# Chunk 5's squares sooner, chunk 1's tokens added on VectorE, and a transposition of the first group copied by ScalarE

## The chip, the core and the metric

The kernel runs on one core of a Trainium2 chip. The core has five engines with queues of their own: TensorE (PE) multiplies matrices into PSUM; VectorE (DVE) does elementwise work, reductions and transpositions of 32x32 blocks; ScalarE (ACT) does activations and copies; GpSimd (POOL) does elementwise work on SBUF; SyncE (SP) issues most of the DMAs. The metric is the device time of one execution in microseconds (us), lower is better. Beside it a profiled execution gives a trace; its span is the time from the first to the last instruction.

## What is computed

Two blocks follow each other. The first is a delta-rule attention over batch 4, 8 heads, 768 tokens and head size 48: a state matrix per head is read with each query, then corrected with each key and value.

```python
k_n = k / (np.linalg.norm(k, axis=-1, keepdims=True) + 1e-06)
for t in range(S):
    y[:, :, t] = np.einsum('bhd,bhde->bhe', q[:, :, t], state)
    v_old = np.einsum('bhde,bhd->bhe', state, kt)
    state = state + bt[:, :, :, None] * np.einsum('bhd,bhe->bhde', kt, vt - v_old)
```

The heads of a token then stand side by side as one row of 384 numbers, 3072 rows in all, and pass a feed-forward network with w_in (384 x 2048) and w_out (2048 x 384), both given in double precision:

```python
h = x @ w_in
g = 0.5 * h * (1.0 + erf(h * inv_sqrt2))
out = g @ w_out
```

## The kernel before

**Tiling.** The 768 tokens are cut into 12 chunks of 64. Two batches of 8 heads make a unit of 128 rows (`tiles[c, a]`, a = 0 and 1, so `NA` is 2), and two chunks make a group. Within a chunk the recurrence becomes a triangular system. Its Gram matrices come from PE (`grams`, L414, copied out by ACT in L425). The 32x32 diagonal blocks of a group are inverted together on DVE: `eliminate_steps` scales (L476, L477), flips (L482, L487), eliminates row after row (L496, L501, L503), and in `back` transposes the result three times: into `XM` (L512) and into the right and left columns of `Zf` (L516). In groups after the first the third of these is a copy by ACT instead (L520). `clear` then sets the lower left block of `Zf` to zero in group 0. The off-diagonal block is joined in two levels of small matmuls: `join` (L548, used for group 0) multiplies one 32x32 block at a time; `join_run` (L593, used for later groups) takes two heads at once and uses only the blocks it needs, in four strided pieces. Level 0 is scaled back into `XM` by DVE (L559 or L605), level 1 goes to `Zf` by ACT (L563 or L572).

**A chunk.** `against_state` multiplies keys and queries with the state (psK, L667), `subtract` forms the right side W (DVE, L678 and L684) and copies the part of the queries to y (ACT, L679), `solve` multiplies with Zf (psU, L702) and ACT copies U out, `use` and `update` form psY (L732, L743). `next_state` adds to the state (DVE, L748), and `read` gets the tokens x out of PSUM: for chunks 0 and 1 ACT copies them (L756), for later chunks DVE adds y in the same step (L758). `turn` transposes x for the network (psX); for chunk 1 it does so with two matmuls per 128 columns that add x and y on the way (L776), otherwise with one transposition (L779).

**Norms.** For chunks from 4 on, `norms` squares the keys on ACT (ksq), and `prep` sums the squares on DVE (L349) and takes the root on POOL (L351). `finish` turns both roots of a group into the factors gm on DVE (L303 to L307), which the group's elimination needs.

**The network.** For chunks 0 and 1 it is plain (psH with a gelu on ACT, L811 and L817 or L902; psO, L829). From chunk 2 on, `part_of_layer` and `second_layer` use fewer products with sums around them (L916, L859); L939, L947, L958 and L968 are DVE's sums between these products, and PE's next product into psY waits for L947. The weights arrive in double precision and are decoded to single by DVE and ACT during chunks 0 and 1: `begin` (L231, L234), `exponents` (L237, or ACT through the helper at L902), `mantissas` (L251, L253), `signed` (L260, L261), which also fetches a later part.

**Order.** Up to L1172 all engines run in the order in which the code is written. After that `plan` gives each step a time in units of chunks; the steps are sorted by it. DVE runs in exactly that order, and so do ACT's instructions that go through `keep` (L902); the others are placed by a scheduler. `together` holds PE's instructions of several steps together.

## Time and profile before

| what | value |
| --- | --- |
| median of 3 executions | 646.0 us (645.03 to 646.12) |
| profiled execution | 644.96 us |
| its span | 643.2 us |
| PE busy | 617.9 us, 96% |
| DVE busy | 496.3 us, 77% |
| ACT busy | 259.9 us, 40% |
| POOL busy | 66.0 us, 10% |
| mean granted clock of TensorE | 0.985 |

In a timeline each row has a start and a duration in us, the engine, the line of the kernel, the operation, what it writes and reads, and in brackets how long the engine had been idle before it and what ended that. Rows of one kind that follow closely are merged (x3), and a matmul counts as two records. In a view of waits the columns are: who waited for whom, us in total, how often, the longest. In a view of windows each row has the stretch, its length, then for PE, the loading of weights, DVE, ACT and POOL the busy time and the number of instructions, then the granted clock, the share of DMA and GB/s. In the clock row of the page each digit is a fortieth of the span, in tenths of full speed.

### The profile page before, as it was taken

To read this page: it belongs to the slowest core of one execution; us is meant where nothing else is said; L and a number is where in the kernel's file an instruction comes from. 1 tells how busy PE (TensorE), PEld (TensorE's weight loads), DVE (VectorE), ACT (ScalarE), POOL (GpSimd) and SP (SyncE) were. 2 spreads that over 40 slices of the span, in tenths; PEclk is the share of its full clock that TensorE was granted. 3 is DMA by queue.
4 is the path that set the end of the run, shared out by engine and by line. 5 is a ranking of instruction groups with operands and counts; after the bars stand their busy time and mean duration, and the time that the engine had idled before them with its cause. 6 is when DMAs were issued, how large, how long until landed. Compare 5 with 4: busy or idle time off the path is not lost.

```text
span 643.2 us, 22156 instructions
## 1 busy us (share of the span) xinstructions
PE 617.9 (96%) x9702; PEld 573.8 (89%) x9702; DVE 496.3 (77%) x1011; ACT 259.9 (40%) x586; POOL 66.0 (10%) x58
## 2 busy tenths in 40 slices
PE   6759999999989999999999999999999999999997
PEld 5658876776879999999999999999999999999997
DVE  6999989989589997999577999577999565354342
ACT  4576767524632256132266132266132253132230
POOL 4044002001301003001003001013001000000000
PEclk9987999999989999999999999999999999999999
DMA  9794683204422335312325312411211400100100
GB/s 135 174 273 159 129 199 113 45 1 74 84 37 42 56 43 91 58 24 37 66 34 86 61 21 41 67 21 33 51 25 35 69 3 3 25 2 3 25 2 24
DMA packets 158433, 39.79 MB, mean 62 GB/s; under 512 B 150016, under 2 KB 153216, under 8 KB 158336
## 3 DMA queue, kind: packets, MB, share of 16 engines
q1 hardware_dynamic: 155664, 37.34, 30.0%
q10 hardware_dynamic: 2672, 1.03, 0.8%
q8 instruction: 76, 1.25, 0.8%
q14 instruction: 21, 0.17, 0.1%
HBM read 33.62 MB, written 4.72 MB: 60 GB/s over the span
## 4 chain that ended last, share of the span: by engine, by line
PE 77%; DVE 14%; DMA 2%; issue 2%; SPq 2%; ACT 1%; POOL 1%; DVEq 0%; POOLq 0%
PE psX L859 12%; PE psY L916 11%; PE psY L859 8%; PE psX L916 8%; PE psV L916 5%; PE psZ L916 5%; PE psZ L859 4%; PE psV L859 4%; PE psK L667 3%; DVE Nu L503 3%; DVE tmp L501 3%; PE psG L414 3%; PE psJ L593 3%; PE psH L811 2%; PE psY L732 2%
## 5 line engine op out<-in xcount | busy, mean ns | idle before, releaser
L916 PE MATMUL psX<-xT,w_in_sb 128*128 128x128 f32 x480 | 64.8, 278 | 0.0
L503 DVE TENSOR_TENSOR Nu<-Nu,tmp 128x58 f32<-128x58 f32 (+13 forms) x168 | 57.9, 344 | 5.8
L501 DVE TENSOR_TENSOR tmp<-Nu 128x58 f32<-128x58 f32 (+13 forms) x168 | 58.0, 345 | 4.4
L916 PEld LDWEIGHTS psX<-xT,w_in_sb 128*128 128x128 f32 x480 | 59.4, 193 | 0.9
L902 ACT COPY xT<-psX 128x768 f32<-128x768 f32 x9 | 7.2, 799 | 124.3 <-PE psX L788 124.3
L351 POOL TENSOR_TENSOR n<-n,half 128x16 f32<-128x16 f32 x10 | 31.4, 3145 | 251.8 <-DVE n L349 191.2
L859 PE MATMUL psX<-w_out_sb,G 128*128 128x192 f32 x320 | 55.3, 326 | 0.0
L859 PEld LDWEIGHTS psX<-w_out_sb,G 128*128 128x128 f32 x320 | 52.1, 190 | 0.0
L811 PE MATMUL psH<-xT,w_in_sb 128*128 128x256 f32 x192 | 45.2, 390 | 0.5 <-ACT G L902 0.4
L829 PE MATMUL psO<-w_out_sb,G 128*128 128x384 f32 x128 | 43.9, 490 | 0.0
L811 PEld LDWEIGHTS psH<-xT,w_in_sb 128*128 128x128 f32 x192 | 36.3, 193 | 8.0 <-ACT G L902 1.3
L916 PE MATMUL psY<-xT,w_in_sb 128*128 128x128 f32 x320 | 43.1, 279 | 0.0
L916 PEld LDWEIGHTS psY<-xT,w_in_sb 128*128 128x128 f32 x320 | 39.8, 196 | 0.0
L902 ACT COPY pu<-psZ 128x512 f32<-128x512 f32 x40 | 23.5, 587 | 39.3 <-PE psZ L916 37.7
L829 PEld LDWEIGHTS psO<-w_out_sb,G 128*128 128x128 f32 x128 | 23.6, 190 | 14.0
L902 ACT ACTIVATE G<-G 128x512 f32<-128x512 f32 x40 | 25.2, 630 | 23.3 <-DVE G L947 22.6
L939 DVE TENSOR_TENSOR psY<-psY,pu 128x512 f32<-128x512 f32 x20 | 14.0, 698 | 22.4 <-PE psY L916 19.6
L376 POOL TENSOR_TENSOR V<-V,n 128x384 f32<-128x384 f32 x18 | 17.0, 959 | 135.4 <-DMA V<-in_v_dram 115.5
L859 PE MATMUL psZ<-T,pu 128*128 128x192 f32 x160 | 28.6, 332 | 0.0
L859 PE MATMUL psY<-T,G 128*128 128x192 f32 x160 | 28.6, 332 | 0.0
L859 PE MATMUL psV<-w_out_sb,G 128*128 128x192 f32 x160 | 27.7, 326 | 0.0
L859 PE MATMUL psX<-T,G 128*128 128x192 f32 x160 | 27.6, 326 | 0.0
(183 smaller groups left out, 1346.1 us busy)
## 6 DMA issues: line engine op xcount, KB each, us to landing
Kp<-in_k_dram SPq DMA_DIRECT2D x76, 96.0 KB, 3.2
w_out_sb<-in_moe_w_in_dram SPq DMA_DIRECT2D x24, 256.0 KB, 4.1
w_raw<-in_moe_w_out_dram SPq DMA_DIRECT2D x16, 384.0 KB, 4.5
V<-in_v_dram SPq DMA_DIRECT2D x48, 96.0 KB, 3.1
out_dram<-o_sb SPq DMA_DIRECT2D x40, 96.0 KB, 2.2
Qp<-in_q_dram SPq DMA_DIRECT2D x64, 32.0 KB, 2.1
Qp<-in_q_dram SPq DMA_DIRECT2D x16, 96.0 KB, 4.7
Qp<-in_k_dram SPq DMA_DIRECT2D x32, 32.0 KB, 2.2
```

What stands on the lines that cost most here:

```text
L351: nc.gpsimd.tensor_tensor(flat, flat, half, op=ALU.pow)
L376: engine.tensor_tensor(u.V, u.V, ns[u.c][:, u.a].unsqueeze(2).to_broadcast([128, H, D]), op=ALU.mult)
L414: nc.tensor.matmul(psG[HALF[p], r, i * NP + j, :], lhsT=u.Kt[rows, p, j, :], rhs=(u.Qt if x else u.Kt)[rows, p, j, :], start=True, stop=True)
L501: nc.vector.tensor_tensor(tmp, nu[:, j + 1:, j:j + 1].to_broadcast([128, n, j]), nu[:, j:j + 1, 0:j].to_broadcast([128, n, j]), op=ALU.mult)
L503: nc.vector.tensor_tensor(nu[:, j + 1:, 0:j], nu[:, j + 1:, 0:j], tmp, op=ALU.add)
L593: nc.tensor.matmul(psJ[HALF[p], k, :], lhsT=(xm if level else off)[rows, us, :], rhs=zf[rows, us, HB:C] if level else xm[rows, us, :], sta ...
L667: nc.tensor.matmul(u.psK[to, x, r, j, :], lhsT=(u.Qt if x else u.Kt)[rows, p, j, :], rhs=St[rows, u.a, p ^ r, j, :], start=True, stop=True)
L811: nc.tensor.matmul(psH, lhsT=w_in_sb[:, f // 2, m, f % 2 * 128:(f % 2 + 1) * 128], rhs=xTs[c][:, m, :], start=(m == 0), stop=(m == NM - 1))
L829: nc.tensor.matmul(u.psO, lhsT=G[:, u.a, f, :], rhs=w_out_sb[:, f, :], start=(f == 0), stop=(f == NF - 1))
L859: nc.tensor.matmul(ps_, lhsT=lhs[:, f, :], rhs=rhs[:, f, :], start=first and f == 0, stop=f == FH - 1, skip_group_check=not first)
L902: i = fn(*args, **kw)
L916: nc.tensor.matmul(ps_[:, i], lhsT=lhs[:, f // 2, f % 2 * 128:(f % 2 + 1) * 128], rhs=rhs, start=first and i == 0, stop=True, skip_group_c ...
```

## The change

Three things change.

- The third transposition of group 0 on DVE is left out. `turned_corner` copies the upper left block of `Zf` from its right columns on ACT instead, for chunk 0 before its second join level and for chunk 1 at time 1.05.
- Chunk 1's joins go through `join_run`, two heads at a time, with four instructions on DVE and four on ACT. Chunk 1's tokens are read as in later chunks: DVE adds y to them, and `turn` transposes once. For that the queries' product with the state is written to the partitions of the later chunks.
- Chunk 5's `norms` moves from time 3.06 to 2.93, and its `prep` from 3.06 to 2.961. In ACT's order the two squares now stand right behind the copies of xT of chunk 2, ahead of the Gram copies of chunk 4; in DVE's order the two sums stand ahead of L939 and L968. On SP, the loads of the keys of chunk 6 then stand ahead of one block load instead of behind it.

```diff
+    def turned_corner(c):
+        us = slice(c * NA * H, (c + 1) * NA * H)
+        for p in range(2):
+            top = slice(p * C, p * C + HB)
+            nc.scalar.copy(Zf[0][top, us, 0:HB], Zf[0][top, us, HB:C])
...
-                    psJ = small[0].tile([128, 512], F32, tag="sq" if level else "z", name="psJ")
+                    psJ = small[0].tile([128, 512], F32, tag="sq" if level or g == 0 else "z",
+                                        name="psJ")
...
-                        put_off("join", zf[p * C:p * C + HB, us, HB:C], src)
+                        put = put_off if g else lambda name, to, at: nc.scalar.copy(to, at)
+                        put("join", zf[p * C:p * C + HB, us, HB:C], src)
...
-                        to = HALF[p ^ (j % 2)] if x and u.c > 1 else HALF[p]
+                        to = HALF[p ^ (j % 2)] if x and u.c > 0 else HALF[p]
...
-            if u.c < 2:
+            if u.c < 1:
                 copy(dst, src)
...
-            if u.c == 1:
-
-                for i, part in enumerate((u.x, u.y)):
-                    nc.tensor.matmul(psX[:, m, :], lhsT=part.rearrange("q h d -> q (h d)")[:, cols],
-                                     rhs=ident, start=i == 0, stop=i == 1)
-            else:
-                nc.tensor.transpose(psX[:, m, :], u.x.rearrange("q h d -> q (h d)")[:, cols], ident)
+            nc.tensor.transpose(psX[:, m, :], u.x.rearrange("q h d -> q (h d)")[:, cols], ident)
...
     for a in range(NA):
         join(0, (a,), 0)
-    back2[0](*back2[1:])
+    turned_corner(0)
...
-             [(t, (join, 0, range(NA, 2 * NA), level)) for level, t in enumerate((1.085, 1.16))],
+             at(1.05, 1.051, [(1.0, turned_corner, 1)]),
+             [(1.085, (join_run, 0, range(NA, 2 * NA), ())),
+              (1.16, (join_run, 0, (), range(NA, 2 * NA)))],
...
-                         at(w + 0.06, w + 0.061, [(1.0, norms, 5), (1.0, prep, 5)]),
+                         at(w - 0.07, w - 0.069, [(1.0, norms, 5)]), at(w - 0.039, w - 0.038, [(1.0, prep, 5)]),
```

## The prediction

> **What bounds the kernel now.** I read the page first: how busy each engine is, and at which clock.

> ```profile
> span 643.2 us, 22156 instructions
> ...
> PE 617.9 (96%) x9702; PEld 573.8 (89%) x9702; DVE 496.3 (77%) x1011; ACT 259.9 (40%) x586; POOL 66.0 (10%) x58
> ...
> PEclk9987999999989999999999999999999999999999
> ```

> TensorE (PE) carries the time; the dips of the clock row (a slice is 16.1 us) say that it was slowed around 32 to 64 us and near 180. Then the waits of PE, longest first. After the start-up loads they are few, and from 180 us to the end none above 0.2 us is listed, so whatever PE gains before 180 us stays gained unless VectorE (DVE) then fails to keep up.

> ```profile
> PE psY L916 <- DVE G L947: 4.0, 1, 4.0
> ...
> PE psJ L548 <- DVE XM L559: 2.0, 2, 1.5
> ...
> PE psJ L593 <- DVE XM L512: 0.5, 1, 0.5
> ```

> The 4.0 us wait, in the timeline:

> ```profile
> 169.84 0.94 ACT L902 ACTIVATE ksq<-Kp 128x384 f32<-128x384 f32 x2
> ...
> 170.40 1.01 DVE L349 TENSOR_REDUCE n<-ksq 128x8 f32<-128x384 f32 x2 [0.30 <-ACT ksq L902]
> ...
> 171.33 1.75 DVE L842 TENSOR_TENSOR T<-w_out_sb,T 128x1536 f32<-128x1536 f32 x1
> ...
> 171.49 4.35 POOL L351 TENSOR_TENSOR n<-n,half 128x16 f32<-128x16 f32 x1 [10.76 <-DMA Kp<-in_k_dram]
> ...
> 175.87 0.18 DVE L303 TENSOR_SCALAR n<-n 128x32 f32<-128x32 f32 x1 [2.79 <-POOL n L351]
> ...
> 179.27 0.68 DVE L947 TENSOR_TENSOR G<-psY,pu 128x512 f32<-128x512 f32 x1
> ...
> 180.01 1.56 PE L916 MATMUL psY<-TX,w_in_sb 128*128 128x128 f32 x8 [4.00 <-DVE G L947]
> ```

> Chunk 5's squares (ksq) run on ScalarE (ACT) behind chunk 4's Gram copies; their sums, then the square root on GpSimd (POOL), follow; DVE stands 2.79 us before L303, and L947, whose psY was ready at 173.35 (172.29 + 1.06), queues behind. PE waits for L947. (The DMA named at POOL's row is a load of the next chunk; what released it is the sum that ends at 171.41.) The windows around it show the second price:

> ```profile
> 177.20:180.60 3.40, 0.59 (x5) 0.59 (x6) 3.33 (x5) 0.61 (x2) 0.60 (x1) 1.00 0.43 50
> 180.60:184.00 3.40, 3.40 (x19) 3.40 (x18) 3.33 (x5) 1.09 (x3) 0.00 (x0) 0.50 0.38 45
> ```

> After a stretch with PE busy 0.59 of 3.40 us the clock is 0.50 for 3.4 us. The 24 records from 180.01 take 4.41 us (the next group starts at 184.42); at 0.1115 each (8 in 0.89 later on) they are 2.68. So the wait costs 4.0 + 1.7 = 5.7.

> The other edits sit where PE and DVE are balanced:

> ```profile
> 45.00 1.94 DVE L516 STREAM_TRANSPOSE Zf<-Nu 128x1024 f32<-128x1024 f32 x1
> ...
> 63.51 0.35 ACT L902 ACTIVATE G<-psH 128x256 f32<-128x256 f32 x1
> ...
> 86.79 0.56 DVE L748 TENSOR_TENSOR St<-St,psY 128x384 f32<-128x384 f32 x1 [1.21 <-PE psY L743]
> ...
> 87.72 0.56 DVE L748 TENSOR_TENSOR St<-St,psY 128x384 f32<-128x384 f32 x1 [0.38 <-PE psY L743]
> ...
> 132.14 5.32 PE L829 MATMUL psO<-w_out_sb,G 128*128 128x384 f32 x16
> ...
> 135.71 2.09 DVE L512 STREAM_TRANSPOSE XM<-Nu 128x1024 f32<-128x1024 f32 x1
> ...
> 137.95 1.15 PE L593 MATMUL psJ<-XM,G 32*64 32x64 f32 x32 [0.48 <-DVE XM L512]
> ```

> At 87.7 DVE waits for PE. From there to 137.8 DVE decodes weights and eliminates without a gap above 0.21 us, and PE waits for it at 137.95. From 138 to 176 PE runs without a wait.

> [...] half for about 3.4 us after the 4.0 us wait, and for four windows from 44.5 to 58.1. [...] The root takes 2.90 us at 157.82 and 4.35 beside L842 at 171.49[...].

> **Squares sooner.** Nothing is removed: two squares (0.94), two sums (1.01) and one root move. ACT's order has the squares right after xT's second copy (162.62 + 0.48 = 163.1); ACT then idles until 164.56, so they end at 164.05 in its gap. Their input was loaded by issues at 149.6 to 153.5, a median 3.2 us to landing. On DVE the sums now stand behind L846 (ends 165.83): 166.85, in the 2.77 us before L939 at 168.60. The root then ends between 169.8 (2.90) and 171.2 (4.35). DVE goes L939, L968 (to 170.1), L842 (1.75, to 171.85), L303 at once: 4.0 earlier than 175.87. L947 ends at 179.95 - 4.0 = 175.95, and PE's preceding psV ends at 176.0. The wait closes and the dip with it: **-5.7**. POOL's queue holds nothing between the two roots. On SP the loads into the same K buffers, 171.00 before, no longer wait for the squares, and one block load goes behind them; PE waits for neither.
> Will DVE keep up? It starts 4.0 earlier, PE 5.7. Its next idle times are 0.93 (before L939 at 186.48) and 0.38 (L678 at 190.25); absorbed, it is 5.3 earlier. Its next hand-over is XM, ready at 228.36 for a PE that comes at 228.77: 0.4 spare. 5.7 - 5.3 = 0.4: just enough, cost 0 to 0.4; I take 0.

> **Third transposition.** DVE loses 1.94 us at 45.00. ACT gets four copies 32x512 (0.62 each, by diag<-G L425): two between 43.2 and 45.32, where it waited 2.30 us for psJ, and two behind the exponents that end at 56.2, before the gelu that PE releases at 58.34. Cost nothing there; without that cover 1.24 each pair. POOL's clearing starts about 1.2 sooner, but psU (47.76) needs ACT's clearing too, which ends 47.66 as before: no gain for chunk 0. DVE's decoding runs about 1.6 earlier (exponents on ACT at 54.50 hold the rest). So exponents of part 3 on ACT go from 61.50 to 60.03 (behind the gelu 59.64 + 0.39), end 62.17; L261 62.2 to 63.15.

> **Joins in pairs.** 32 records of 64 columns for 64 of 32: 1.15 for 1.20, nothing. DVE 4 x 0.43 = 1.74 (L605) for 1.41: +0.33. ACT 1.49 for 1.17, in idle time before the next gelu. XM then ends at 63.17 + 1.74 = 64.9 instead of 66.08, and PE, whose tile before it no longer waits behind ACT, is 1.1 earlier up to 86.5 (0.5 to 1.6).

> **Chunk 1's tokens.** PE drops 12 psX matmuls pairwise (1.34 per tile) for 3 transpositions (about 0.3): -2.1. ACT drops 6 copies, 1.96. DVE gets 6 adds, by L758 1.08 per tile, and behind them stands the decoding. At 87.7 DVE now does St, adds, St, adds: 85.65 + 2 x 1.58 (by 157.66 to 160.80) = 88.8 to 88.95, before 88.28. **+0.7** (0.2 to 1.3), carried by the full DVE queue to XM: 138.5 instead of 137.81. ACT's exponents, now behind earlier gelus, are within 0.1 of DVE's need once; 0 to 0.5 more.
> What is late next: PE would be done at 137.46 - 1.1 - 2.1 = 134.3, so it stands 3.5 to 4 us before this join, as long as the wait that vanishes at 176. If a clock window falls mostly into it, up to 3.4 us at half follow: 0 to 1.7. [...] I take half of it, **+0.9**, as what a median of executions sees.

> Sum against its own time (span 643.2, execution 644.96): -5.7 + 0.7 + 0.9 = -4.1, span 639.1, execution 640.9. That execution lies 1.04 under the median 646.0 of runs spread over 1.1[...]; from the median: **641.9**.

> **Rivals.**
> - *Full gain:* the stall before group 1's join doesn't slow the clock and DVE's lateness is 0.2. Speaks for it: earlier holes of 2 us left the clock at 1.00. 646.0 - 5.5 = 640.5.
> - *Small gain:* the dip comes whole, ACT's exponents add 0.5, DVE at 228 lags 0.4, adds 1.3: -5.7 + 1.3 + 0.5 + 0.4 + 1.7 = -1.8, 644.2. All ends at once; each is possible.
> - *It doesn't do what it says:* the root isn't what holds L947. Then only the start-up moves, and the 4.0 us of slack at 176 swallow it: 645.5 to 646.5. Against: the chain of waits passes root, L303, L947 in a row.
> - *Slower:* the clock stays at half after group 1's join for several windows, as it did for four at 44.5, because small matmuls (psJ, psK) follow the stall. PE is the bound from 138 on, so each window costs 1.7. It decides from three windows (5.1 against a net gain of 5.0); with four 646.0 - 5.0 + 6.8 = 647.8. Against: psO's large matmuls follow 3.1 us later.

> **How the numbers follow.** Forecast 0.58 (641.9, its own range 640.8 to 643.4), full gain 0.14, small gain 0.13, no change 0.06, slower 0.09. Below 0.2% (1.3 us) this kernel's measurement can't tell a change. Faster by more: 0.58 + 0.14 + 0.13 = 0.85; within: 0.06; slower 0.09. The range takes forecast, full and small gain: 639.8 to 644.6; left out are no change and slower, 0.15.

> **What would show it.** Squares right: POOL's root of chunk 5 before 168, L303 about 4 us sooner in its stage, no PE wait at L947's product and clock 1.00 after it. Transposition and joins: PE's psJ of chunk 1 near 65, the state update of chunk 1 near 85.6. Tokens: XM of group 1 0.2 to 1.3 later than 137.8, PE waiting 3 to 4 us there, the clock row telling whether a dip follows. The prediction is wrong if DVE reaches that join earlier than before, if a new PE wait above 1 us stands at 228, or if L303 still waits for POOL.

## The result, and the profile after

The changed kernel takes 644.32 us in the median of 14 runs (642.56 to 646.57) where the kernel before takes 645.78 (645.03 to 646.63): a ratio of 0.9973, 95% interval 0.9963 to 0.9982, so 1.5 us faster. The forecast was 641.9, 4.1 faster. The direction was right, the gain about a third of the forecast. The runs of the changed kernel spread over 4.0 us, those of the kernel before over 1.6.

The profiled execution took 644.23 us, 0.73 less than that of before (644.96). The page, first the lines that answer those of before:

```profile
span 642.5 us, 21992 instructions
...
PE 619.7 (96%) x9620; PEld 574.2 (89%) x9620; DVE 496.9 (77%) x1018; ACT 260.1 (40%) x586; POOL 64.5 (10%) x58
...
PEclk9567999989999999999999999999999999999999
```

PE is busy 1.8 us more than before, though it has 82 instructions fewer. PE's products take longer at half clock (32 records of psK 1.07 to 1.10 us there, 0.65 to 0.68 at full): the dip near 180 us (the twelfth slice of the row) is gone, but one has come in the ninth slice, 129 to 145 us. The lower digits of the start-up are no slower start-up: four transpositions of psT take 1.11 us from 20.38 us here and 1.11 us from 19.77 us before, at half the pace of those at 37.65 us before and 38.75 us here (a record every 0.21 and every 0.11 us). The trace of before names no clock ahead of its first change at 33.8 us, and its row shows full digits there. So the mean clocks of the two executions, 0.985 and 0.962, can't be compared. The waits of PE, whole span:

```profile
PE psJ L600 <- DVE XM L512: 2.9, 1, 2.9
...
PE psG L414 <- issue: 1.7, 2, 1.2
```

Before, the longest wait after the start-up was that for L947's product (L949 now), 4.0 us. It is no longer in the list. In its place stands the wait of group 1's join for XM, 2.9 us instead of 0.5. One of the two waits named "issue" (the engine waited for nothing that the profile shows) lies at 250 us; it returns below.

The stage of chunk 5's squares in the timeline (start, length, engine, line, operation):

```profile
167.22 0.94 ACT L904 ACTIVATE ksq<-Kp 128x384 f32<-128x384 f32 x2
...
169.97 1.01 DVE L349 TENSOR_REDUCE n<-ksq 128x8 f32<-128x384 f32 x2
...
171.05 2.90 POOL L351 TENSOR_TENSOR n<-n,half 128x16 f32<-128x16 f32 x1 [6.10 <-DVE n L349]
175.90 0.18 DVE L303 TENSOR_SCALAR n<-n 128x32 f32<-128x32 f32 x1
...
179.30 0.68 DVE L949 TENSOR_TENSOR G<-psY,pu 128x512 f32<-128x512 f32 x1
...
180.07 1.12 PE L918 MATMUL psY<-TX,w_in_sb 128*128 128x128 f32 x8
```

These clock times look like those of before, 175.9 for L303 and 180.1 for PE. But PE came to this stage 4.2 us later (the product at 164.36 before starts at 168.59 now), so relative to its stage everything here is 4.2 us sooner: the root ends 1.95 us ahead of L303, which doesn't wait, and PE doesn't wait for L949. In the windows from 177.20 to 184.00 PE is busy 3.40 of each 3.40 us at clock 1.00. So the part of the change with the largest price did all that was expected of it; the loss lies ahead of it, at group 1's join, where two small products follow each other, psJ (the join) and psK (keys and queries with the state):

```profile
130.80 5.32 PE L831 MATMUL psO<-w_out_sb,G 128*128 128x384 f32 x16
139.07 1.64 PE L600 MATMUL psJ<-XM,G 32*64 32x64 f32 x32 [2.95 <-DVE XM L512]
140.64 1.10 PE L675 MATMUL psK<-St,Kt 48*64 48x48 f32 x32
141.53 1.07 PE L675 MATMUL psK<-St,Qt 48*64 48x48 f32 x32
142.38 1.07 PE L675 MATMUL psK<-St,Kt 48*64 48x48 f32 x32
143.24 1.07 PE L675 MATMUL psK<-St,Qt 48*64 48x48 f32 x32
144.24 3.87 PE L831 MATMUL psO<-w_out_sb,G 128*128 128x384 f32 x8
148.03 0.27 PE L600 MATMUL psJ<-Zf,XM 32*64 32x64 f32 x1
```

Before, the same steps started at 137.95 (psJ, 1.15), 139.02 (psK), 141.03 (psO, 2.85) and 143.81. The join comes 1.12 us later, and from it to the next one PE needs 8.96 us instead of 5.86. The windows, laid along the clock's own steps, say why (columns: length, then busy time of PE, of its weight loads, of DVE, ACT and POOL, the granted clock, and the DMA share and rate):

```profile
136.10:139.51 3.41, 0.46 (x16) 0.47 (x17) 3.31 (x6) 0.00 (x0) 0.00 (x0) 1.00 0.00 0
139.51:142.92 3.41, 3.41 (x110) 3.29 (x108) 3.27 (x6) 2.09 (x2) 0.00 (x0) 0.50 0.02 5
142.92:146.33 3.41, 3.41 (x56) 2.41 (x53) 2.05 (x2) 0.00 (x0) 0.00 (x0) 0.50 0.02 5
146.33:149.75 3.42, 3.42 (x72) 2.27 (x71) 0.45 (x2) 0.44 (x2) 0.00 (x0) 1.00 0.00 0
```

After a window in which PE stood for 2.95 us there are two windows at half clock, not one: 6.83 us, in which 3.1 us of work is lost. At 168 us the changed kernel is 4.2 us behind the kernel before; the squares give 5.8 back by 217 us (220.80 for a DVE sum that stood at 222.40).

Of these 1.6 us, 0.8 go once more, in the middle of a block of Gram products:

```profile
247.88 1.15 PE L600 MATMUL psJ<-Zf,XM 32*64 32x64 f32 x32
248.96 1.14 PE L414 MATMUL psG<-Kt 48*64 48x64 f32 x58
250.62 0.34 PE L414 MATMUL psG<-Kt 48*64 48x64 f32 x6 [0.51 <-issue]
250.88 1.41 PE L861 MATMUL psZ<-T,pu 128*128 128x192 f32 x7
```

The block of 64 records stops after 58, and the next product starts 1.92 us after the block's start instead of 1.09. From there to the end the lead of 0.73 to 0.8 us doesn't move. The sum in the trace: 1.1 later at the join, 3.1 in the dip, -5.8 at the squares, 0.8 in the gap, -0.8 in all, which is what the two profiled executions differ by.

### The profile page after: what moved, and what is told of

It is laid out like the page before. It is cut to its first block, busy times and chain, and to the rows that moved or that the text cites. A ratio compares the mean times of both kernels' runs of the same rounds, so it can differ in the third digit from the quotient of the medians.

```text
span 642.5 us, 21992 instructions
## 1 busy us (share of the span) xinstructions
PE 619.7 (96%) x9620; PEld 574.2 (89%) x9620; DVE 496.9 (77%) x1018; ACT 260.1 (40%) x586; POOL 64.5 (10%) x58
## 4 chain that ended last, share of the span: by engine, by line
PE 84%; DVE 9%; ACT 2%; issue 2%; DMA 1%; POOL 0%; SPq 0%; POOLq 0%
PE psX L861 12%; PE psY L918 11%; PE psX L918 9%; PE psY L861 8%; PE psV L918 6%; PE psZ L918 6%; PE psG L414 5%; PE psZ L861 4%; PE psV L861 4%; PE psK L675 4%; PE psJ L600 3%; PE psO L831 3%; PE psU L710 2%; PE psY L740 2%; PE psH L813 2%
## 5 line engine op out<-in xcount | busy, mean ns | idle before, releaser
L501 DVE TENSOR_TENSOR tmp<-Nu 128x58 f32<-128x58 f32 (+13 forms) x168 | 58.1, 346 | 4.4
L351 POOL TENSOR_TENSOR n<-n,half 128x16 f32<-128x16 f32 x10 | 30.6, 3060 | 250.3 <-DVE n L349 200.9
L831 PE MATMUL psO<-w_out_sb,G 128*128 128x384 f32 x128 | 45.5, 501 | 0.2 <-DVE w_out_sb L261 0.2
```

The source lines that it names most:

```text
L351: nc.gpsimd.tensor_tensor(flat, flat, half, op=ALU.pow)
L501: nc.vector.tensor_tensor(tmp, nu[:, j + 1:, j:j + 1].to_broadcast([128, n, j]), nu[:, j:j + 1, 0:j].to_broadcast([128, n, j]), op=ALU.mult)
L831: nc.tensor.matmul(u.psO, lhsT=G[:, u.a, f, :], rhs=w_out_sb[:, f, :], start=(f == 0), stop=(f == NF - 1))
```

## The experiments

All times are medians, and each ratio is to the kernel before as it was timed beside the experiment: 646.23 us for the first four, 645.80 for the filling with four matmuls, the wide matmuls, the third transposition and the later join, 646.61 for the rest. The changed kernel's 644.32 stands beside a kernel before of 645.78. Experiments of different groups are best compared by their ratios.

**Squares alone.** In the kernel before, the one line of the plan.

```diff
-at(w + 0.06, w + 0.061, [(1.0, norms, 5), (1.0, prep, 5)]),
+at(w - 0.07, w - 0.069, [(1.0, norms, 5)]), at(w - 0.039, w - 0.038, [(1.0, prep, 5)]),
```

> The kernel before with chunk 5's squares moved sooner, and nothing else. Theory (the squares are worth their 5.7 us, and the other edits gave 4.2 us of it back at group 1's join): 640.1 us, between 639.5 and 640.8; no wait of PE at 176 to 180 us, a wait of about 0.5 us at group 1's join near 139 us, and full clock from 60 us on. Rival (the 4.0 us wait of PE is passed on to a later wait, and the squares are worth little alone): 644.0 to 645.0.

Measured: 640.0 us (639.5 to 640.86), ratio 0.9904 (0.9884 to 0.9924). The waits of PE from 66 to 640 us are two, and the windows of the two places are all at full clock:

```profile
PE psJ L593 <- DVE XM L512: 0.5, 1, 0.5
PE psJ L548 <- DVE XM L559: 0.5, 1, 0.5
```

```profile
136.10:139.50 3.40, 2.92 (x76) 2.03 (x78) 3.38 (x2) 0.00 (x0) 0.00 (x0) 1.00 0.00 0
...
177.20:180.60 3.40, 3.40 (x33) 3.40 (x33) 3.23 (x8) 2.28 (x5) 0.00 (x0) 1.00 0.38 48
```

What follows: the price of 5.7 us was right. One line of the change is better than the whole of it by some 4 us.

**All but the squares.** The changed kernel with that line as before.

> The changed kernel with chunk 5's squares back at their old place. Theory (the other edits cost about 4.2 us ahead of 150 us, and the chain squares, root, scale hangs on ACT's copies that follow PE, so it moves with PE and swallows nothing): 649.0 to 650.5 us, two stretches at half clock, after 139 us and after 180 us. Rival (the chain behind the squares keeps its time, so the 4.0 us wait swallows the lateness): 645.5 to 646.5.

Measured: 650.11 us (648.21 to 653.43), ratio 1.0057 (1.0036 to 1.0078). PE waits 2.99 us for XM, half clock follows for 3.4 us, and then it waits 4.00 us for L949 and runs at half for two windows more. The chain behind the squares moved with PE and swallowed nothing. The other edits together make the kernel 3.7 us slower.

**Tokens as before.** The changed kernel with chunk 1's tokens copied by ACT and summed in the transposition.

```diff
-            if u.c < 1:
+            if u.c < 2:
                 copy(dst, src)
...
-            nc.tensor.transpose(psX[:, m, :], u.x.rearrange("q h d -> q (h d)")[:, cols], ident)
+            if u.c == 1:
+                for i, part in enumerate((u.x, u.y)):
+                    nc.tensor.matmul(psX[:, m, :], lhsT=part.rearrange("q h d -> q (h d)")[:, cols],
+                                     rhs=ident, start=i == 0, stop=i == 1)
+            else:
+                nc.tensor.transpose(psX[:, m, :], u.x.rearrange("q h d -> q (h d)")[:, cols], ident)
```

> The changed kernel with chunk 1's tokens as before (copies on ACT, the sum made by TensorE in the double transposition). Theory (the three token additions, 2.7 us of DVE, are what makes XM late): XM ends before 137 us, PE's wait at group 1's join is under 1.5 us with no half clock behind it, 639.8 to 641.0 us. Rival (the lateness comes from the joins in pairs or from the third transposition): the wait stays at 2.5 us or more, half clock follows, 643.5 to 645.0.

Measured: 639.96 us (639.53 to 640.5), ratio 0.9899 (0.9881 to 0.9917). First two lines of the changed kernel, the first sum of chunk 1's state and XM's transposition, then two of this one, the same sum and the join:

```profile
86.23 0.56 DVE L756 TENSOR_TENSOR St<-St,psY 128x384 f32<-128x384 f32 x1 [1.21 <-PE psY L751]
...
136.95 1.97 DVE L512 STREAM_TRANSPOSE XM<-Nu 128x1024 f32<-128x1024 f32 x1
```

```profile
86.90 0.56 DVE L756 TENSOR_TENSOR St<-St,psY 128x384 f32<-128x384 f32 x1 [1.22 <-PE psY L751]
...
138.07 1.15 PE L600 MATMUL psJ<-XM,G 32*64 32x64 f32 x32 [0.50 <-DVE XM L512]
```

PE's wait at the join is 0.50 us, without half clock. One point missed: the join starts at 138.07, so XM ended only about 138 us and not before 137. The wait is short because PE arrives at 137.57 instead of 136.12: twelve matmuls stand again in place of six transpositions, and the start-up of this execution was 0.7 us slower (chunk 1's second join at 66.27 for 65.61). The tokens act from both sides, DVE later and PE sooner, and what grows is the gap between them. The start-up can be taken out by counting from that first state sum, which waits for PE. With the tokens on ACT and TensorE, XM's transposition starts 48.92 us after it in all three traces (before, squares alone, and this one, at 135.82); with the tokens on DVE 50.68 to 50.74 us in nine traces, and 51.40 in the tenth, where DVE waits 0.6 us for a load. PE arrives at the join 50.67 or 50.68 us after it in the three, and 49.89 in the changed kernel. So the tokens make XM 1.8 us later and PE 0.8 sooner; the transposition itself is 0.1 us shorter, and the wait grows from 0.48 to 2.95. From the state sum on the other edits of the first group add nothing.

**The wait filled with work of no use**, eight matmuls and then four.

```diff
+        if g == 1 and ts0 and not ts1:
+            for i in range(8):        # 4 in the second
+                nc.tensor.matmul(sets[0][2].rearrange("q k n -> q (k n)")[:, 0:384],
+                                 lhsT=w_out_sb[:, i, 0:128], rhs=w_out_sb[:, i, 0:384],
+                                 start=True, stop=True)
         for k in range(H):
```

> The changed kernel with eight 128x384 matmuls of no use put into the wait ahead of group 1's join, into a tile that the join then overwrites: 8 x 0.332 = 2.66 us of work in a wait of 2.95. XM is as late as before. Theory (the wait drops the clock for two windows, which costs 3.2 us): no half clock after 139 us, 640.5 to 641.8 us. Rival (the small matmuls of the join and of psK bring the half clock, or are slow by themselves): half clock stays, psJ takes 1.6 and psK 3.6 us, 644.0 to 645.0.

Measured: 643.14 us (642.56 to 643.32), ratio 0.9945 (0.9929 to 0.9962). No half clock, psJ at 1.15 and the psK at 0.65 to 0.68, but the time was missed, because the filling was mis-sized: a matmul of this shape leaves two records of 0.332 us, so eight took 5.3 us, 2.4 more than the wait, and the join came 2.1 us later (141.14). A gap of 0.67 us in psK adds to it, of the kind that the last two experiments are about. Therefore four:

> As the filled wait, with four matmuls of no use in place of eight: each 128x384 matmul leaves two records of 0.332 us, so eight took 5.3 us, 2.3 more than the wait of 2.95; four take 2.66 and fit. Theory (without the half clock the changed kernel is 3.2 us faster, and the eight cost 2.3 of it): 640.3 to 641.5 us, group 1's join about 139 us, no half clock behind it, runs within 1.5 us of each other. Rival (the filling is not what freed the clock, or costs by itself): 642.5 us or more.

Measured: 640.77 us (640.0 to 641.36), ratio 0.9922 (0.991 to 0.9934).

```profile
130.36 5.32 PE L836 MATMUL psO<-w_out_sb,G 128*128 128x384 f32 x16
135.52 2.74 PE L597 MATMUL psJ<-w_out_sb 128*128 128x384 f32 x8
138.74 1.15 PE L605 MATMUL psJ<-XM,G 32*64 32x64 f32 x32 [0.48 <-DVE XM L512]
```

```profile
136.10:139.50 3.40, 2.92 (x33) 1.74 (x33) 3.33 (x5) 0.00 (x0) 0.00 (x0) 1.00 0.00 0
139.50:142.90 3.40, 3.40 (x144) 2.81 (x141) 3.28 (x6) 2.09 (x2) 0.00 (x0) 1.00 0.02 5
```

The join is hardly sooner than in the changed kernel (138.74 and 139.07), PE has 2.7 us of work more, and the kernel is about 3.3 us faster (0.9922 for 0.9973). That is the experiment on the dip: it is the idle time that costs, by the clock behind it, and not the join's or psK's size alone, which run here at their full rate. (0.8 of the 3.3 are the gap in the Gram block, which this kernel doesn't have.) The spread of the runs falls with it, from 4.0 us in 14 runs to 1.4 in 5.

**Half of the filling**, two matmuls.

> As the filled wait with two matmuls of no use (1.33 us) in the wait of 2.95, so that about 1.6 us of wait are left. Theory (half clock follows when a window of 3.41 us was idle for most of it, as the two that were followed by it were, 2.95 and 2.81 us of 3.4; 1.6 us is too short): no half clock, 640.4 to 641.5 us. Rival (any wait of more than a microsecond brings it): half clock for one or two windows, 642.0 to 644.5 us.

Measured: 642.31 us (640.97 to 644.47), ratio 0.9944 (0.9925 to 0.9962): neither expectation. In the profiled execution PE waits 1.70 us and the clock stays full.

```profile
138.75 1.15 PE L605 MATMUL psJ<-XM,G 32*64 32x64 f32 x32 [1.70 <-DVE XM L512]
```

The six runs stand in two groups, three at 640.97 to 641.28 and three at 643.34 to 644.47. In this trace the wait is split between two of the clock's windows, in which PE is still busy 2.17 and 2.95 us. Had it fallen into one, 1.71 us of work would have been left there, and windows with 1.69 and 1.89 us of work were followed by half clock in other traces (see the section on the hardware). So a wait of 1.7 us may bring the dip in some executions and not in others, if the windows' edges lie otherwise over it, as they do from trace to trace (by 2.7 us at this join, same section); the runs of the second group have no trace, and their mean clocks on record (0.970 to 0.988) don't differ from those of the first (0.966 to 0.989), so this is argued and not shown.

**Wide matmuls behind the join.** The wait stays; four matmuls of the second layer stand between psJ and psK instead of behind psK.

```diff
-             at(2.6, 2.601, [(1.0, together, (against_state, third))]),
+             at(2.653, 2.6531, [(1.0, together, (against_state, third))]),
-             at(2.65, 2.651, [(1.0, sum_of_w_in, 1)]),
+             at(2.655, 2.656, [(1.0, sum_of_w_in, 1)]),
```

> The changed kernel with the same four 128x384 matmuls between group 1's join and psK in place of behind psK: the wait of 2.95 us on XM stays. Theory (the clock comes back only after a window of 3.41 us with wide matmuls in it; behind the join stood psJ and psK alone, 64x64 and 64x48): half clock for one window, 3.4 us, in place of two, 642.2 to 643.6 us, and the runs lie closer together than 4 us. Rival (what fills the window does not matter): two windows, 643.9 to 644.8 us.

Measured: 643.09 us (641.36 to 643.62), ratio 0.9956 (0.9942 to 0.9969), about 1.1 us less than the changed kernel by the ratios, with intervals that overlap a little, and a spread of 2.3. PE waits 2.96 us, and one window is at half:

```profile
137.90:141.31 3.41, 1.69 (x34) 1.52 (x35) 3.38 (x3) 0.01 (x1) 0.00 (x0) 1.00 0.02 5
141.31:144.73 3.42, 3.42 (x6) 1.69 (x6) 3.30 (x6) 2.07 (x2) 0.00 (x0) 0.50 0.00 0
144.73:148.14 3.41, 3.41 (x194) 2.92 (x192) 0.82 (x1) 0.00 (x0) 0.00 (x0) 1.00 0.02 5
```

This speaks for the theory, but the windows of this execution also lie otherwise over the wait, so one trace doesn't settle it. The section on the hardware puts all traced dips beside each other.

**The third transposition on DVE again.**

```diff
-    turned_corner(0)
+    back2[0](*back2[1:])
...
-             at(1.05, 1.051, [(1.0, turned_corner, 1)]),
```

> The changed kernel with the first group's third transposition on DVE again (1.9 us of DVE for four ACT copies of 0.62 us). Theory (it gave DVE 1.6 us before 65 us, and of this nothing reaches group 1's join in full): XM later by 0 to 1.6 us, the wait on XM longer by as much, 644.3 to 646.0 us. Rival (the start-up's half clock is what the ACT copies bring, and it costs 0.6 us there): 643.2 to 643.9 us and no half clock between 13 and 37 us.

Measured: 645.47 us in 13 runs (643.6 to 646.68), ratio 0.9989 (0.9979 to 1.0). XM's transposition starts at 137.55 instead of 136.95; PE comes as much later, waits 2.96 us as before, and here the half clock lasts three windows:

```profile
138.92:142.33 3.41, 2.62 (x60) 2.54 (x64) 3.03 (x4) 0.95 (x1) 0.00 (x0) 0.50 0.02 5
142.33:145.75 3.42, 3.42 (x113) 3.28 (x107) 3.31 (x5) 1.13 (x2) 0.00 (x0) 0.50 0.00 0
145.75:149.16 3.41, 3.41 (x6) 1.69 (x5) 0.22 (x1) 0.00 (x0) 0.00 (x0) 0.50 0.02 5
```

The 0.6 us are not the edit's: the first sum of chunk 1's state is as much later here (86.86 for 86.23), and in the kernel of the wide matmuls, which has the ACT copies, it stands at 86.78 and XM's transposition at 137.47. The times don't tell the edit from nothing either (0.9979 to 1.0, and 0.9963 to 0.9982 for the changed kernel). The rival's half clock in the start-up fails too: the row shows none here, but neither does it in the kernel filled with eight, which has the ACT copies. With the tokens as before, squares alone and squares with both edits of the first group take the same 640.0.

**The joins not in pairs.**

```diff
-             [(1.085, (join_run, 0, range(NA, 2 * NA), ())),
-              (1.16, (join_run, 0, (), range(NA, 2 * NA)))],
+             [(t, (join, 0, range(NA, 2 * NA), level)) for level, t in enumerate((1.085, 1.16))],
```

> The changed kernel with the first group's two joins for chunk 1 not in pairs (64 matmuls 32x32 in place of 32 of twice the width, two DVE multiplications of 0.7 us in place of four of 0.44). Theory (the pairs are worth about nothing: their 0.4 us less of PE and 0.3 more of DVE lie before a wait on DVE): XM within 0.4 us of 139.0, the wait about 2.9 us, 643.6 to 645.0 us. Rival (the four short multiplications are a large part of what makes XM late): XM 0.6 us or more sooner, below 643.4 us.

Measured: 644.1 us (642.92 to 645.8), ratio 0.9962 (0.9948 to 0.9975), not told apart from the changed kernel (0.9963 to 0.9982). XM came later here (137.87 for the start of L512), not sooner, 0.6 of it a wait of DVE for a load of the weights. The pairs are worth nothing that these runs can show.

**The join later.** In the changed kernel, group 1's join and psK behind four more of the matmuls that had stood behind psK.

```diff
-             at(2.595, 2.596, [(1.0, together, join1[0])]),
+             at(2.6525, 2.6526, [(1.0, together, join1[0])]),
```

with the two lines of the wide matmuls above.

> The changed kernel with group 1's join and chunk 2's psK behind four more of the second layer's 128x384 matmuls, which stood between psK and the next joins (2.66 us). No work is added; DVE's order is unchanged. Theory (the wait is filled by work that has to be done anyway, 2.66 us, and with it goes the half clock, 3.2 us): 637.9 to 639.3 us, PE's wait on XM at most 0.5 us. Rival (the next joins, now straight behind psK, wait for DVE's multiplication of the first, and the wait is only moved): 641.5 us or more, a wait of 1.5 us or more at the second join.

Measured: 639.89 us (639.38 to 640.14), ratio 0.991 (0.9896 to 0.9923). The wait is 0.45 us and the clock is full, as expected, yet 0.6 us or more were missing. At 228 us this kernel was 1.1 us ahead of squares alone (a DVE sum at 228.24 and at 229.35), at 268 us 0.3 behind. Its waits of PE between 66 and 640 us say where:

```profile
PE psG L414 <- issue: 1.1, 1, 1.1
...
PE psJ L600 <- issue: 0.4, 1, 0.4
```

The gap in the Gram block is there again, behind the 58th record, and longer. It is in all five traced kernels that have the changed one's number of PE instructions, always behind the 58th record (0.40 to 1.07 us), and behind the 54th with the four records of the half filling; it is not in those with 8, 16, 18, 64 or 82 records more. The 58th and the 54th are the same place when PE's matmul records are counted from the start of the trace: 3774 stand ahead of the gap in all six.

**The later join, shifted by 8 records.** Four matmuls 128x64 of no use ahead of the join.

```diff
+            for i in range(4):
+                nc.tensor.matmul(sets[0][2].rearrange("q k n -> q (k n)")[:, 0:64],
+                                 lhsT=w_out_sb[:, i, 0:128], rhs=w_out_sb[:, i, 0:64],
+                                 start=True, stop=True)
```

> The later join with four matmuls of no use, 128x64, ahead of group 1's join (8 records, about 0.3 us in all, in a wait of 0.45): it moves every later instruction of PE 8 records down in the program. Theory (the gap of 0.4 to 1.1 us in the middle of a psG block near 250 us, at its 58th record in every kernel with the changed one's count of PE instructions and in no kernel with 8, 16, 18 or 82 more, belongs to a place in PE's instruction stream): no such gap between 160 and 300 us, 638.3 to 639.2 us. Rival (the gap belongs to the moment or to the data, not to the place): the gap of 0.4 us or more stays, 639.6 to 640.2 us.

Measured: 638.94 us (638.53 to 639.33), ratio 0.9883 (0.987 to 0.9896), the lowest median here. It was not timed beside squares alone (0.9904, 0.9884 to 0.9924), and the intervals overlap. The Gram block is whole and the next product follows 1.09 us after its start:

```profile
244.90 1.16 PE L414 MATMUL psG<-Kt 48*64 48x64 f32 x64
245.99 2.87 PE L866 MATMUL psZ<-T,pu 128*128 128x192 f32 x16
```

At the other place of the kernel the gap moved instead of going:

```profile
142.07 0.58 PE L680 MATMUL psK<-St,Qt 48*64 48x48 f32 x25
143.64 0.33 PE L680 MATMUL psK<-St,Qt 48*64 48x48 f32 x7 [0.99 <-issue]
```

With four matmuls of no use the ratio is 0.9883 and not 0.991. The gaps explain only a part of that: the profiled executions differ by 0.5 us (639.80 and 639.33), as the gaps do, 1.07 and 0.37 us there and 0.99 here. What the traces show is that the gaps belong to places in PE's instruction stream, not to the moment or the data.

## Why the prediction was wrong

**The squares, -5.7: right.** The trace of the changed kernel gives -5.8, the squares alone -6.2 (4.9 to 7.5). ACT, DVE and POOL did as written: the root in 2.90 us, L303 without a wait, PE without a wait. At 228 us no new wait of PE appeared, as taken.

**DVE later at the join, +0.7: right in kind, low in size.** Measured +1.1 in the trace, within the 0.2 to 1.3 stated. The tokens cost DVE about what was foretold: 1.8 us from chunk 1's first state sum on, less the 1.1 us by which the start-up was to be sooner. The start-up was only 0.56 sooner in this execution (that sum at 86.23; 85.70 to 86.86 in all ten kernels with the tokens on DVE, 86.66 to 86.90 in the other three). At the end of the kernel the same is seen, if not clear of noise: with the wait filled the ratio is 0.9922, and 0.9904 for squares alone, 1.2 us apart. The stall was foretold as 3.5 to 4 us (the prediction's own 138.5 less 134.3 would be 4.2) and was 2.95: PE was only 1.35 us sooner (136.12 for 137.46) and not 3.2. Half a microsecond of that is the start-up. The other is the tokens: from psY to the join PE is 0.8 us shorter and not 2.1. Its psX is shorter as counted, but it then works on psO and psH in turns, with a wait of 0.17 us for decoded weights, where it had psO in one stretch; the rest was not taken apart.

**The clock behind the stall, +0.9: this step failed.** It read "0 to 1.7", one window at most, half of which was taken. In the traced execution it cost 3.1 us, two windows. Two assumptions in it were wrong. It let the clock come back after one busy window, although the rival on the slower side named the reason why it may not: behind the stall stand psJ and psK. That rival was set aside because "psO's large matmuls follow 3.1 us later". At full clock they do; at half clock psJ and psK take 5.2 us, 3.4 of them the whole first window. And it took the mean of "a dip or none" where the stall, at 2.95 of 3.41 us, is so long that a dip followed each time: all five traced kernels with a stall of 2.9 us or more at this join have one, of one to three windows, and in one of these kernels PE was still busy for 1.89 us of the window ahead of the dip. (The four windows at half that the prediction saw from 44.5 to 58.1 us lie at 44.1 to 57.7 in the trace; their number is right.)

**A term that wasn't in the sum, +0.8.** The gap in PE's stream at 250 us is not in the kernel before, and nothing in its profile tells of it. With -5.8, +1.1, +3.1 and +0.8 the sum is -0.8, the difference of the two executions; the medians of the runs differ by more, 1.5, because the profiled execution of before was 0.8 us below its median and that of the changed kernel 0.1. How many windows at half the other executions have wasn't traced.

**The edits that were costed at nothing.** The third transposition was free on ACT, and no run shows that it gains anything at the join. The paired joins are free. PE's 2.1 us from the tokens were rightly not counted as a gain, since PE waits for DVE; the 0.8 that came of them lengthen the stall.

**The rivals.** *Small gain* came to 644.2 and the measurement to 644.3, but by luck, with another sum: it had 1.7 for the dip, 0.5 for ACT's exponents and 0.4 at 228 us, of which only the dip came, almost twice as large, and it had nothing for the gap near 250 us. *Slower* named what the trace then showed, psJ and psK behind the stall and more than one window at half, and needed three; three were seen once, in the kernel with the third transposition on DVE, which no longer differs from the kernel before by an amount that can be told. *Full gain* (640.5) is what the other edits spoil: squares alone reach it.

## What to carry to other kernels

Price a stall of TensorE with the clock behind it, and look at what stands in the queue there: in these traces a stall that left PE 1.89 us of work or less in a window of 3.41 us was followed by half clock, small matmuls in that half clock were slower (32 records of psK took 1.07 to 1.10 us for 0.65 to 0.68), and a window of them with 0.5 us of wide ones or less was followed by another at half. Before work is moved from TensorE to the engine that it waits for next, compare the two arrival times at their next meeting; work taken from the engine that arrives first buys nothing, and may cost. Bundled edits should be timed one by one: here one line held all of the gain.

## What the runs showed of the hardware

| kernel, start of the window (us) | PE busy of 3.41 us | with | next window |
|---|---|---|---|
| before, 180.61 | whole | 128x128 | full |
| wide matmuls behind the join, 141.31 | whole | 128x384 | full |
| third on DVE, 145.75 | whole | 128x384 | full |
| joins not in pairs, 144.70 | whole | 128x384 | full |
| all but squares, 185.04 | whole | 128x128 | full |
| all but squares, 140.67 | whole | psK, then 1.2 us of 128x384 | full |
| changed, 142.92 | whole | 1.4 us of psK, then 128x384 | full |
| changed, 139.51 | whole | psJ, psK | half |
| third on DVE, 142.33 | whole | psK, then 0.5 us of 128x384 | half |
| joins not in pairs, 141.29 | whole | psK, then 0.1 us of 128x384 | half |
| third on DVE, 138.92 | 2.62 | psJ, psK | half |
| all but squares, 181.63 | 2.63 | 128x128 | half |

The window filled with psJ and psK alone (139.51) was followed by half clock, as was one of 128x128 matmuls with 0.78 us of idle time at its start (181.63); 1.2 us of wide matmuls behind psK sufficed once, 0.5 us didn't. At full clock the small tiles didn't lower it: in the join moved later PE ran psJ and psK alone from 138.60 to 141.7, and the clock stayed at 1.00. What separates the two outcomes was not tried.

**Gaps tied to places in the program.** In runs of small matmuls, whose records follow each other every 15 to 35 ns, PE stopped for 0.3 to 1.1 us at two places of its instruction stream. Ten such gaps stand in the traces: six behind PE's record 3774, counted from the start, and four behind record 1865 (the kernel filled with eight, the tokens as before, the later join and the later join shifted). Moving the stream by 8 records took the gap out of the Gram block, and the other one moved from psJ into psK.

The trace also shows reads of 16 KB, on a queue that it names "instruction", at the second place seven of them 3.9 to 6.9 us apart (223.92 to 258.18 us of the changed kernel). There the gap ends at 250.62 us, 1.41 behind the end of the 29th of these reads (249.21), and the kernel before, which has no gap, comes to record 3774 at 249.71, 3.98 us behind the end of its own (245.73). All six gaps at the second place end 1.3 to 1.5 us after the end of the 29th read, and all four at the first place 1.2 to 1.5 us after the end of the 14th. The seven kernels without a gap at the second place come there 1.8 us or more after the 29th read's end. In the kernel filled with four the first place falls among wide matmuls, 1.4 us after the read, and the record comes only 0.2 us late. That PE waits there for a load of instructions is the author's estimate from these times; no run changed the reads, so it is not shown.
